# The skip term of an S4D convolution: VectorE adds for groups of chunks in place of TensorE products for each chunk

## The chip, the cores and the metric

The kernel runs on one core of a Trainium2 chip. A core has a matrix engine (TensorE, in the profile PE, its weight loads PEld), VectorE (DVE), ScalarE (ACT), GpSimd (POOL), and a queue engine that issues most transfers (SyncE, SP). Every engine works through its own list of instructions in order; an instruction that needs something of another engine or of a transfer waits on a semaphore, and all that stands behind it on its engine waits too. The metric is the device time of one execution in microseconds, as the median of several runs; a profiled execution gives the trace.

## The reference

A block of a conditioned sequence model: sequence length 2048, width D = 640, 128 complex states per channel, feed-forward width 1728, batch 1, all float32. Cut to what matters:

```python
def ssm(u, log_A_real, A_imag, C_real, C_imag, log_dt, D_skip):   # u: [1, L, D]
    dt = exp(log_dt)
    A = -exp(log_A_real) + 1j * A_imag                            # [D, N]
    C = (C_real + 1j * C_imag) * dt[:, None]
    K = 2 * einsum("dn,dnl->dl", C, exp((A * dt[:, None])[:, :, None] * arange(L))).real
    y = irfft(rfft(u_t, 2 * L) * rfft(K, 2 * L))[..., :L]         # causal convolution
    return y_t + u * D_skip

sa, ca, ga, sb, cb, gb = split(silu(c) @ w_mod, 6)
h = layernorm(x) * (1 + ca) + sa
x = x + ga * ssm(h, ...)
h = layernorm(x) * (1 + cb) + sb
x = x + gb * ((silu(h @ w1) * (h @ w3)) @ w2)
```

The skip term `u * D_skip` is the same as adding `D_skip` to the convolution kernel K at time 0, channel by channel. That is how the kernel does it, before and after the change: it adds `D_skip` to one element of each channel's generated kernel.

## The kernel before

The 640 channels are five blocks of 128 (b = 0 to 4), and a block is eight chunks of 16 channels (c = 0 to 7). For each chunk the convolution kernel K is generated on the chip:

- GpSimd adds up phases as integers (`ph`, task `g{b}.{c}.ph`) and multiplies magnitudes (`yy`, `xx`, tasks `z0` to `z2`).
- ScalarE takes sines and cosines (`tr`, tasks `s0` to `s4`), VectorE multiplies them in (`yy`, `xx`, tasks `m0` to `m4`).
- TensorE sums over the states into PSUM (`kps`, 128 x 256, task `p`, the function `product` inside `gen_chunk`): 64 small products. Then come four more products, each of a 32 x 32 identity with four columns of the table `dsk`, which add `D_skip` to column 63 of each of the chunk's four 64-column groups. `kps` has one buffer.
- ScalarE copies `kps` to the chunk's 256 columns of the block's table `ks` in SBUF (task `r`, function `rows`).

`ks` goes through a two-stage Fourier transform by matmuls. The first stage is eight tasks `k{b}.{i}.m` for a block (in the profile `ps<-wk,ks`, 16 passes each); task i reads the columns of chunk i. Its result is copied to `sp` by VectorE or ScalarE (task `e`). The second stage is `fk`. The normalized input takes a parallel road: `hn`, `hb`, a store to device memory (`hs<-hb`), a load in another layout (`xb<-hs`), the same first stage (`ps<-wk,xb`) and a second one, `fh`. The spectra are multiplied (`hz`, `fp`) and go back by `fz`, `zt` and further transfers (`zd`, `iz`). All this ends near 331 us; the feed-forward part takes the rest, and is bound by TensorE.

`dsk` is a 128 x 160 table, zero but for four partitions, that is filled once near the start by four small loads on SyncE's queue, after the loads of x, of the modulation weights (`sp<-in_w_mod`) and of two constant tables.

What sets the order: each step is a task with an engine and the names of the tasks it needs (`Plan.add`). One long table of numbers, `ORDER`, lists the tasks in the order of issue (an accent picks the second of two engines); `Plan.sequence` checks it against the needs and `InOrder` keeps each engine to it, so that nothing is rearranged later. All instructions that go through `InOrder` show its line, L151. ScalarE also has other work in these lists: squares for the layernorm statistics (`xs<-xs,h_nm`), and for each block five exponentials (`late<-late`) with a table load ahead and another behind.

Of the kernel before, what the change touches and what calls it, by code (L numbers as in the profile page):

```python
# [10 lines left out]
F32 = mybir.dt.float32  # L11
F32R = mybir.dt.float32r
I32 = mybir.dt.int32
AF = mybir.ActivationFunctionType
# [4 lines left out]
P = 128  # L19
# [6 lines left out]
NB = 5  # L26
E4 = P // 4
# [7 lines left out]
1 80 78 81 79 82 83 150' 2 4 19 42 20 41 14 21 15 84 22 43 23 44 16 85 151 24 17 25 26 45 46 18 28 59 47 30 27 29 48 96 33 36 49  # L35
34 5 111 35 32 61 31 37 40 50 51 38 39 3 152' 153 156 6 7 8 52 53 62 60 157 154 10 91 158 155 159 167 168 89 86 120 93 87 95 107
54 121 13 310 105 109 98 169 171 113 172 173 110 106 90 174 55 102 100 88 56 114 176 118 177 183 179 66 170 117 178 184 185 57 104
58 64 187 188 108 175 99 189 180 181 67 186 192 194 9 115 193 103 190 160 92 199 200 201 101 97 203 11 195 68 202 161 182 204 191
215 122 123 208 65 63 209 196 197 69 205 206 210 116 94 207 211 219 112 138 124 127 198 162 212 71 213 128 134 400' 119 163 125
# [3 lines left out]
267 338 334 259 339 315 265 266 405 260 268 77 335' 409 72 147 148 149 0 550 340 272 273 269 274 270 271 261 275 322 330 279 276  # L43
555 283 280 281 288 341' 551' 262 282 284 285 323 286 331 290 552 289 553 318 277 326 556 319 287 291 327' 417 421 418 422 278 320
321 423 292 557 426 545 316 293 137 410 75 74 546 424 419 558 420 427 317' 428 547 548 328 413' 414 324 429 425 294 329 430 433
437 325 346 342 344 554 559 436 434 442 435 431 347 438 444 343 345' 443 348 350 365 352 439 549 440 441 432 445 449 450 451 452
# [12 lines left out]
730 752 753 608 399 630 826 744 745 618 757 756 827 754 631 755 619 641 759 750 763 764 758 620' 760 766 765 767 768 746 769 770  # L59
# [2088 lines left out]
```

## Time and profile before

| | before |
|---|---|
| median of 3 runs | 940.48 us (939.96 to 941.41) |
| the profiled execution's own time | 940.2 us |
| its span | 938.4 us |
| mean granted TensorE clock | 0.983 |
| instructions | 21120 |
| TensorE busy | 856.7 us (91%) |
| VectorE busy | 693.8 us (74%) |
| ScalarE busy | 539.7 us (58%) |
| GpSimd busy | 342.3 us (36%) |
| share of the chain that ended last: TensorE, VectorE, transfers, ScalarE, GpSimd | 70%, 12%, 6%, 5%, 3% |

The shares are means over the whole span, and the two parts of the program are unlike: up to about 331 us all engines are busy with the convolution, after about 375 us TensorE alone is. So the tables by stretch, and the chain of waits piece by piece, say more than the busy shares. In a row of the timeline stand the start and the length of an instruction or a run of like ones (us), engine, line, operation, output and inputs, and in brackets how long the engine stood before it and what released it. A row of the chain has start, length, engine or transfer, output.

### The profile page before, as it was taken

The page shows a single profiled execution, that of the slowest core. Times are in us where ns is not written, and L with a number is a line of the kernel's source. Part 1 is how long each engine was busy: PE and PEld are TensorE (multiplying, and loading weights), DVE is VectorE, ACT ScalarE, POOL GpSimd, SP SyncE. Part 2 cuts the span into 40 slices and gives each one's busy share as a digit, 9 for nine tenths or more (in the row PEclk, how much of TensorE's full clock was granted, in tenths as well). Part 3 has the DMA queues.
Part 4 walks back from the last instruction along what each step waited for, and adds up shares of the span by engine and source line. Part 5 has one row for each costly group of instructions (what it writes and reads, how often), then busy time and mean ns, then how long its engine had stood idle before and what let it go on. Part 6 is the DMA issues. An engine that isn't in the chain of part 4 may idle for free.

```text
span 938.4 us, 21120 instructions
## 1 busy us (share of the span) xinstructions
PE 856.7 (91%) x8309; PEld 679.0 (72%) x8309; DVE 693.8 (74%) x1310; ACT 539.7 (58%) x1032; POOL 342.3 (36%) x370
## 2 busy tenths in 40 slices
PE   1167999999999986999999999999999999999997
PEld 1035857878888873787777778878788888888776
DVE  7998999999989977897677676668656464646523
ACT  6789999989787741754344454446444444444311
POOL 0899989998998500002121121000121212120000
PEclk9987999999999998999999999999999999999999
DMA  9976563525143598655354322275532323230274
GB/s 206 267 236 166 160 156 108 135 81 128 48 110 88 137 242 210 167 183 168 110 157 126 116 82 70 85 229 190 148 106 74 95 75 94 73 96 29 90 244 144
DMA packets 110124, 127.40 MB, mean 136 GB/s; under 512 B 10697, under 2 KB 89801, under 8 KB 108745
## 3 DMA queue, kind: packets, MB, share of 16 engines
q1 hardware_dynamic: 108552, 124.88, 46.5%
q8 instruction: 65, 1.06, 0.5%
q10 hardware_dynamic: 1472, 1.18, 0.5%
q14 instruction: 35, 0.28, 0.1%
HBM read 95.89 MB, written 30.15 MB: 134 GB/s over the span
## 4 chain that ended last, share of the span: by engine, by line
PE 70%; DVE 12%; DMA 6%; ACT 5%; POOL 3%; issue 2%; SPq 1%; ACTq 0%; DVEq 0%; POOLq 0%
PE c L151 19%; PE acc L151 17%; PE X L151 12%; PE ps L151 5%; PE fz L151 4%; PE kps L151 3%; PE fk L151 3%; PE fh L151 3%; PE gu L151 2%; DMA zd<-zt 1%; DVE xb L151 1%; PE iy L151 1%; DVE yy L151 1%; DVE xx L151 1%; DMA sp<-zd 1%
## 5 line engine op out<-in xcount | busy, mean ns | idle before, releaser
L151 PE MATMUL acc<-w,ah 128*128 128x512 f32 x448 | 137.0, 391 | 0.8 <-DMA w<-w2d 0.8
L151 ACT ACTIVATE tr<-ph 128x512 f32<-128x512 int32 (+1 forms) x160 | 93.7, 599 | 6.9 <-DVE yy L151 3.6
L151 PEld LDWEIGHTS acc<-w,ah 128*128 128x128 f32 x448 | 83.4, 188 | 18.1 <-ACT ah L596 1.2
L597 DVE TENSOR_TENSOR wl<-s,wh 128x256 fp32r<-128x256 f32 x92 | 39.0, 424 | 65.3 <-ACT wh L596 65.0
L151 PE MATMUL acc<-w,al 128*128 128x512 f32 x208 | 81.3, 391 | 2.0 <-DVE al L597 2.0
L773 POOL TENSOR_TENSOR s<-wr 128x256 f32<-128x256 f32 x22 | 16.5, 748 | 179.2 <-DVE wl L597 111.2
L596 ACT ACTIVATE wh<-s 128x256 fp32r<-128x256 f32 x92 | 37.8, 410 | 75.9 <-PE X L151 56.8
L151 POOL TENSOR_TENSOR ph<-p,p 128x1024 int32<-128x1024 int32 x40 | 78.7, 1968 | 4.7 <-ACT tr L151 4.1
L596 ACT ACTIVATE wh<-wr 128x256 fp32r<-128x256 f32 x92 | 38.3, 418 | 52.2 <-PE X L151 40.1
L774 POOL TENSOR_TENSOR s<-s,wr 128x256 f32<-128x256 f32 x22 | 17.0, 772 | 131.1 <-issue 131.0
L834 ACT ACTIVATE t<-g 128x512 f32<-128x512 f32 x44 | 27.8, 632 | 55.1 <-DVE g L798 55.0
L151 DVE TENSOR_TENSOR yy<-yy,tr 128x512 f32<-128x512 f32 (+1 forms) x60 | 56.6, 945 | 2.8 <-ACT tr L151 1.8
L803 DVE SCALAR_TENSOR_TENSOR g<-t,g 128x512 f32<-128x512 f32 x48 | 33.7, 702 | 31.3 <-ACT t L834 29.4
L151 DVE TENSOR_TENSOR xx<-tr,xx 128x512 f32<-128x512 f32 x80 | 54.2, 681 | 2.3 <-ACT tr L151 1.8
L151 PE MATMUL fz<-fp,wz 64*128 64x512 f32 x224 | 54.1, 608 | 0.4 <-DVE fp L151 0.4
L151 PE MATMUL kps<-yy,xx 128*32 128x64 f32 x1920 | 37.3, 229 | 17.3 <-DVE xx L151 14.2
L151 PEld LDWEIGHTS kps<-yy,xx 128*32 128x32 f32 x1920 | 32.3, 113 | 27.1 <-issue 10.3
L597 DVE TENSOR_TENSOR wl<-wr,wh 128x256 fp32r<-128x256 f32 x92 | 40.5, 441 | 14.4 <-ACT wh L596 14.3
L151 PE MATMUL ps<-wk,xb 128*64 128x128 f32 x640 | 47.5, 294 | 2.9 <-DVE hb L151 0.9
L151 PEld LDWEIGHTS ps<-wk,xb 128*64 128x64 f32 x640 | 43.3, 220 | 5.3 <-issue 1.4
L151 PEld LDWEIGHTS acc<-w,al 128*128 128x128 f32 x208 | 39.0, 188 | 11.1 <-DVE al L597 2.9
L775 POOL TENSOR_TENSOR s<-wr 128x256 f32<-128x256 f32 x22 | 16.9, 769 | 79.8 <-DVE wl L151 48.4
(464 smaller groups left out, 2473.8 us busy)
## 6 DMA issues: line engine op xcount, KB each, us to landing
w<-w2d SPq DMA_DIRECT2D x42, 640.0 KB, 3.9
wr<-in_w SPq DMA_DIRECT2D x50, 320.0 KB, 3.6
zd<-zt SPq DMA_DIRECT2D x40, 256.0 KB, 3.3
w2d<-w SPq DMA_DIRECT2D x14, 640.0 KB, 3.4
xs<-in_x SPq DMA_DIRECT2D x16, 320.0 KB, 11.8
hs<-hb SPq DMA_DIRECT2D x20, 256.0 KB, 3.4
xb<-hs SPq DMA_DIRECT2D x20, 256.0 KB, 4.7
iz<-zd SPq DMA_DIRECT2D x32, 160.0 KB, 4.1
```

The source lines that it names most:

```text
L151: self.prev = self.k.order(f(*a, **kw), self.prev)
L596: self.nc.scalar.activation(H, v, AF.Copy)
L597: eng.tensor_tensor(Lo, v, H.bitcast(F32), op=ALU.subtract)
L773: eng.tensor_tensor(s[0], u[:, 0:2], u[:, 2:4], op=ALU.add)
L774: eng.tensor_tensor(s[1], s[0], g[:, 0:2], op=ALU.subtract)
L775: eng.tensor_tensor(s[2], g[:, 0:2], u[:, 0:2], op=ALU.subtract)
L803: V.scalar_tensor_tensor(g, th, 1.0, g, op0=ALU.add, op1=ALU.mult)
L834: tanh = lambda o, i: A.activation(o, i, AF.Tanh, scale=0.5)
```

## The change

- The four identity products of each chunk go, and the dependence of the chunk's `p` on the `dsk` loads with them.
- `kps` and a new row of 160 columns share one PSUM buffer, `small` (128 x 512): columns 256 to 511 are `kps`, columns 0 to 159 the row.
- A new ScalarE task `dskp` copies the whole table `dsk` to that row, once, after its four loads.
- New VectorE tasks `d{b}.{c}` add the row's columns to column 63 of the 64-column groups of `ks`, for several chunks at once; c is the last chunk of the group. The table `SKIPS` gives the groups: chunks 0 to 3, 4, 5 to 7 in block 0; 0 to 3, 4 to 6, 7 in blocks 1 and 2; 0 to 3, 4 and 5, 6, 7 in blocks 3 and 4. That makes 17 additions of 128 x 16, 12, 8 or 4 elements. Each needs the copies `r` of all chunks of its group, and `dskp`.
- The first-stage transform of a chunk needs its group's addition, where it needed the chunk's own copy.
- `ORDER` is written anew, because the new tasks shift the numbers. Decoded to names, all old tasks stand in their old order on every engine.

```diff
+SKIPS = (((0, 3), (4, 4), (5, 7)), ((0, 3), (4, 6), (7, 7)), ((0, 3), (4, 6), (7, 7)), ((0, 3), (4, 5), (6, 6), (7, 7)), ((0, 3), (4, 5), (6, 6), (7, 7)))
...
-            for q in range(4):
-                g = slice(32 * q, 32 * q + 32)
-                nc.tensor.matmul(kps.rearrange("p (e b) -> p e b", b=64)[g, :, 63], self.ident[g, g], self.dsk[g, d0 // P, d0 % P // 4:d0 % P // 4 + 4],
-                                 start=False, stop=True, skip_group_check=True, tile_position=(32 * q, 32 * q))
...
+        self.small = psg.tile([P, 512], F32, name="small", tag="kg", bufs=1)
...
-                kps[c] = self.psg.tile([P, 256], F32, name=f"kps{b}{c}", tag="kg", bufs=1)
+                kps[c] = self.small[:, 256:]
...
-            add(n + "p", "PE", 1.3, lambda c=c: ch[c][4](), [n + f"m{i}" for i in range(5)] + (["dsk"] if b == 0 else []), t + 3,
+            add(n + "p", "PE", 1.3, lambda c=c: ch[c][4](), [n + f"m{i}" for i in range(5)], t + 3,
...
+        def skip(c0, c1):
+            o, d = slice(4 * c0, 4 * c1 + 4), self.small[:, :NB * E4].rearrange("p (b e) -> p b e", b=NB)
+            V.tensor_add(self.ks[b][:, o, 63], self.ks[b][:, o, 63], d[:, b, o])
+        for c0, c1 in SKIPS[b]:
+            add(f"d{b}.{c1}", "DVE", .2, lambda c0=c0, c1=c1: skip(c0, c1), [f"{g}.{c}.r" for c in range(c0, c1 + 1)] + ["dskp"], base(c1) + 4)
...
-            after = [f"g{b}.{i}.r"] if m else [f"h{b}.f"]
+            after = [f"d{b}.{c1}" for c0, c1 in SKIPS[b] if c0 <= i <= c1] if m else [f"h{b}.f"]
...
+        add("dskp", "ACT", .3, lambda: A.activation(self.small[:, :NB * E4], flat(self.dsk), AF.Copy), ["dsk"], 20)
```

Where the new instructions stand (the operation, output and inputs with the tile's running number, and the shape; the helper's line is one further down after the change). On ScalarE, near the start, among sines (`tr`, `ph`) and the squares for the layernorm statistics, before:

```order
L151 ACTIVATE ph_293<-ph_293 128x1024
L151 ACTIVATE xs_243,h_ss<-xs_243,h_nm 128x640 x2
L151 ACTIVATE xs_260,h_ss<-xs_260,h_nm 128x640
L151 ACTIVATE tr_0_336<-ph_293 128x512
L151 ACTIVATE xs_176,h_nm<-xs_176 128x640 x2
```

and now:

```order
L152 ACTIVATE ph_294<-ph_294 128x1024
L152 ACTIVATE small<-dsk 128x160
L152 ACTIVATE xs_244,h_ss<-xs_244,h_nm 128x640 x2
L152 ACTIVATE xs_261,h_ss<-xs_261,h_nm 128x640
L152 ACTIVATE tr_0_338<-ph_294 128x512
L152 ACTIVATE xs_177,h_nm<-xs_177 128x640 x2
```

The copy of the row (`dskp`) stands ahead of the squares. On VectorE, in the first block, where chunk 4's last products (`tr_64` with `yy` and `xx`) and the normalized input (`hn`, `hb`) alternate, before:

```order
L151 TENSOR_TENSOR xx_641<-tr_64_677,xx_641 128x512
L151 TENSOR_TENSOR yy_642<-yy_642,tr_64_680 128x1024
L151 TENSOR_TENSOR hb_763<-hn,rw 128x512
L151 TENSOR_TENSOR xx_641<-tr_64_682,xx_641 128x512
L151 TENSOR_SCALAR hn<-sp,rs_y_h,rs_n_h 128x128 x4
L151 TENSOR_SCALAR p_118<-pB 128x128
L151 TENSOR_TENSOR hn<-hn,rw 128x512
L151 TENSOR_TENSOR hb_830<-hn,rw 128x512
```

and now:

```order
L152 TENSOR_TENSOR xx_628<-tr_64_664,xx_628 128x512
L152 TENSOR_TENSOR yy_629<-yy_629,tr_64_667 128x1024
L152 TENSOR_TENSOR ks_132<-ks_132,small 128x16
L152 TENSOR_TENSOR hb_746<-hn,rw 128x512
L152 TENSOR_TENSOR xx_628<-tr_64_669,xx_628 128x512
L152 TENSOR_SCALAR hn<-sp,rs_y_h,rs_n_h 128x128 x4
L152 TENSOR_TENSOR ks_132<-ks_132,small 128x4
L152 TENSOR_SCALAR p_119<-pB 128x128
L152 TENSOR_TENSOR hn<-hn,rw 128x512
L152 TENSOR_TENSOR hb_809<-hn,rw 128x512
```

The additions for chunks 0 to 3 and for chunk 4 stand ahead of `hb` and of `p`. On VectorE, in the second block, between the products of chunk 7 (`tr_240`) and copies of first-stage results (`sp<-ps`), before:

```order
L151 TENSOR_TENSOR hb_2067<-hn,rw 128x512
L151 COPY sp_917<-ps_2069 128x64x8
L151 TENSOR_TENSOR yy_1880<-yy_1880,tr_240_2055 128x1024
L151 COPY sp<-ps_2164 128x64x8
L151 TENSOR_TENSOR xx_1879<-tr_240_2057,xx_1879 128x512
```

and now:

```order
L152 TENSOR_TENSOR hb_2003<-hn,rw 128x512
L152 COPY sp_896<-ps_2005 128x64x8
L152 TENSOR_TENSOR yy_1821<-yy_1821,tr_240_1991 128x1024
L152 TENSOR_TENSOR ks_1305<-ks_1305,small 128x12
L152 COPY sp<-ps_2096 128x64x8
L152 TENSOR_TENSOR xx_1820<-tr_240_1993,xx_1820 128x512
```

The addition for chunks 4 to 6 stands ahead of the copy of `ps_2096`, which is the first-stage transform of chunk 5.

More of the change, by code (lines that the diff above doesn't have):

```diff
@@ L34 @@
 ORDER = """
[L35 to L38, printed above, removed]
@@ new lines @@
+289 345' 558' 263 283 285 286 327 287 335 291 559 290 560 322 278 330 563 323 288 292 331' 421 425 422 426 279 324 325 427 293 564
+430 552 320 294 138 414 76 75 553 428 423 565 424 431 321' 432 554 555 332 417' 418 328 433 429 295 333 434 298 437 441 329 350 346
+348 561 566 440 438 446 439 435 351 442 448 347 349' 447 352 354 369 356 443 556 444 445 436 449 453 454 455 456 457 458 450 462 469
[3 rows of a table added]
+817 818 549 387 506 391 393 395 507 392 498 1067 814 375 508 518 389 396 511 512 510 499 394 397 589 513 509 500 521 1068 398 590'
@@ new lines @@
+514 577 522 519 661 659 533 520 534 535 581 820 377 819 1069 578 537 515 591 528 527 1070 526 579 582 523 821' 822 823 1072 1071 388
[7 rows of a table added]
+752 625 802 764 763 837 761 638 762 626 648 766 757 770 771 765 627' 767 773 772 774 775 753 776 777 926 644 645 649 629 781 780 768
+646 628 617 650 779 782 778 647 783 786 790 769 791 787 923 789 927 792 1339 639 630 651 795 1340 784 793 642 788 1180 640 797 1341
+796 846 1342 798 847' 840 844 841' 794 785 845' 803 1345' 935 939 936 928 652 944 938 951 937 799 1346 655' 1347 1181 940 643 800
@@ new lines @@
+1367' 1384 1383 1473 1477 1385 1386 1387 1389 1388 1397 1398 1402 1390 1391 1399 1481 1403 1455 1448 1458 1457 1450 1460 1451 1462
+1459 1464 1461 1392 1400 1401 1393 1395 1466 1463 1447 1468 1465 1396 1467 1394 1404 1417 1418 1405 1406 1480 1412 1414 1413 1407
+1475 1408 1415 1409 1469 1470 1416 1482 1419 1427 1429 1420 1421 1428 1483 1410 1432 1433 1434 1430 1431 1422 1443 1489 1435 1436
+1490 1491 1478 1492 1472 1471 1411 1423 1425 1437 1440 1438' 1424 1426 1441 1439 1493 1485 1505 1506 1513 1514 1516 1507 1494 1496
[9 rows of a table added]
```

28 lines of the change are left out of this document (10 added, 18 removed), and 72 rows, old and new, of the table ORDER.

## The prediction

> **What bounds the kernel now.** I read the busy table first, then the windows (engine columns are busy us, the column PEclk the granted clock), then the chain of waits.
>
> ```profile
> PE 856.7 (91%) x8309; PEld 679.0 (72%) x8309; DVE 693.8 (74%) x1310; ACT 539.7 (58%) x1032; POOL 342.3 (36%) x370
> ```
> ```profile
> 47.00:92.00 45.00, 32.15 (x596) 20.19 (x596) 39.89 (x79) 40.57 (x78) 42.93 (x42) 0.82 0.72 203
> ...
> 105.00:127.00 22.00, 20.33 (x442) 16.85 (x444) 20.97 (x27) 19.88 (x38) 18.10 (x16) 1.00 0.41 118
> ...
> 147.00:170.00 23.00, 20.83 (x429) 17.08 (x419) 21.79 (x40) 21.56 (x37) 21.72 (x23) 1.00 0.58 143
> ...
> 375.00:938.00 563.00, 551.88 (x2459) 443.12 (x2457) 356.81 (x713) 251.14 (x503) 66.69 (x88) 1.00 0.40 123
> ```
>
> The 91% for PE is a mean over two different kernels. From 375 us on PE works 551.88 of 563 us and this change touches nothing there: that part moves as a block. All forty chunks lie before 331 us, and there VectorE, ScalarE and GpSimd are as full as PE: 39.89, 40.57 and 42.93 of 45 us against PE's 32.15 in the stretch 47 to 92. So the first third is a chain that changes hands:
>
> ```profile
> 52.03 0.69 DVE x L151
> ...
> 81.22 3.64 DMA hs<-hb
> ...
> 105.05 2.84 PE ps L151 x48
> 107.89 1.27 PE kps L151 x68
> ...
> 325.39 1.29 PE kps L151 x69
> ```
>
> A reader should see two things. PE's `kps` steps, the ones that lose work, lie on the chain only from 107.89 on (that row and the one at 325.39 are the first and last of 24). Before that the chain runs over VectorE, ScalarE and transfers, and those get the new work and the new waits. Since every engine runs its list in order, what counts is less the price of an add than whether its operands are there when its place in the list comes.
>
> **What is removed.** One chunk's four skip products (eight passes) take the step from their start to the next matmul:
>
> ```profile
> 306.56 0.24 PE L151 MATMUL kps<-dsk,ident 32*32 32x4 f32 x8
> 306.73 1.99 PE L151 MATMUL fz<-fp,wz 64*128 64x512 f32 x8
> ```
>
> 306.73 - 306.56 = 0.17 us, so 40 x 0.17 = 6.8 us of PE time, but 24 x 0.17 = 4.1 us on the chain. Four of the 24 lie ahead of the wait at 162 us below, where PE ends up waiting for other engines whatever it did before; I count 20 x 0.17 = 3.4 us, with 0 and 4.1 as ends.
>
> **Term A: ScalarE waits for the skip row to land.** The copy of the row into PSUM (task `dskp`) stands in ScalarE's list after the 34.54 step and ahead of the squares at 37.82, and needs the four `dsk` transfers.
>
> ```profile
> 22.63 3.29 SPq L151 DMA_DIRECT2D sp<-in_w_mod  x3
> 27.07 6.06 SPq L151 DMA_DIRECT2D dsk<-in_d_skip  x4
> ```
> ```profile
> 36.27 1.93 PE L151 MATMUL pm<-sp,sc 128*32 128x512 f32 x8 [12.30 <-DMA sp<-in_w_mod]
> 38.52 1.61 PE L151 MATMUL pm<-sp,sc 128*32 128x512 f32 x8 [0.32 <-DMA sp<-in_w_mod]
> ```
> ```profile
> 40.00:41.00 1.00, 0.77 (x7) 0.42 (x4) 1.00 (x3) 1.00 (x4) 1.00 (x2) 1.00 0.02 8
> ```
> ```profile
> 34.54 1.06 ACT L151 ACTIVATE ph<-ph 128x1024 f32<-128x1024 int32 x1
> 37.82 0.83 ACT L151 ACTIVATE xs<-xs,h_nm 128x640 f32<-128x640 f32 x1 [2.22 <-DVE h_nm L151]
> ...
> 45.81 0.83 ACT L151 ACTIVATE xs<-xs,h_nm 128x640 f32<-128x640 f32 x1 [0.34 <-DVE h_nm L151]
> ```
>
> The `dsk` issues end at 33.13 (27.07 + 6.06), behind three large loads of modulation weights on the same queue. PE's waits date the first two of these: 36.27 and 38.52, so 2.25 us apart; the third comes at about 40.8 and the row behind it. The transfers' share falls to 0.02 in 40 to 41, so little is left by then. Estimate of the landing: 41.2, between 40.3 and 42. The copy takes at most the 0.37 us of a 128x256 one (the 79.55 row below), so the squares begin near 41.5 instead of 37.82: 3.7 us, less the 0.34 us that ScalarE waits at 45.81. VectorE takes it over where it waits for ScalarE, the 52.03 step of the chain. **A = +3.4 us**, 2.5 to 4.2.
>
> [...]
>
> **Term B: the first add waits for chunk 3 of block 0.** The add for chunks 0 to 3 stands between `yy` (74.93) and `hb` (76.05, right behind it), that for chunk 4 ahead of `p` (78.91).
>
> ```profile
> 74.93 1.21 DVE L151 TENSOR_TENSOR yy<-yy,tr 128x1024 f32<-128x1024 f32 x1
> ...
> 76.66 0.68 DVE L151 TENSOR_TENSOR xx<-tr,xx 128x512 f32<-128x512 f32 x1
> ...
> 78.91 0.97 DVE L151 TENSOR_SCALAR p<-pB 128x128 int32<-128x128 int32 x1
> ...
> 81.94 0.69 DVE L151 TENSOR_TENSOR x<-x,tr 128x512 f32<-128x512 f32 x1 [0.74 <-ACT tr L151]
> ...
> 89.23 0.30 DVE L151 TENSOR_SCALAR cols<-pv 128x5 f32<-128x5 f32 x3 [1.73 <-PE pv L151]
> ```
> ```profile
> 75.94 3.71 ACT L151 ACTIVATE late<-late 128x1024 f32<-128x1024 f32 x5
> 79.55 0.37 ACT L151 ACTIVATE ks<-kps 128x256 f32<-128x256 f32 x1
> ```
>
> Chunk 3's copy runs behind five exponentials and ends at 79.92. VectorE reaches the add at 76.05 and stands 3.87 us, plus the add's 0.2: 4.1. Queued behind it are `xx` (chunk 4's last product, now ending near 81.4 instead of 77.3), and `hb`, whose store is the chain's 81.22 step. Chunk 4's `kps` follows `xx`, takes 1.5 us (the 80.02 row below) and its copy 0.37, so it ends near 83.4; the next add's place comes at 78.91 + 4.1 = 83.0: another 0.4, and 0.2 for the add. VectorE is 4.7 us late at `p`. It has 0.74 + 1.73 = 2.5 us of waits before 92, which take some of it if their releasers don't move as well, though the `hb` store precedes them on the chain. Between 2.2 and 4.7 I take the middle: **B = +3.4 us**.
>
> **Terms C, D, E: transforms that wait for an add.** The first-stage kernel transforms (`ps<-wk,ks`) now need the group's add.
>
> ```profile
> 107.20 0.68 DVE L151 SCALAR_TENSOR_TENSOR yy<-yy,tr 128x512 f32<-128x512 f32 x1
> ```
> ```profile
> 162.73 1.05 PE L151 MATMUL ps<-wk,ks 128*64 128x128 f32 x16
> 165.34 1.09 PE L151 MATMUL ps<-wk,ks 128*64 128x128 f32 x16 [1.57 <-ACT ks L151]
> ```
> ```profile
> 163.82 0.69 DVE L151 COPY sp<-ps 128x512 f32<-128x512 f32 x1 [0.17 <-PE ps L151]
> ```
> ```profile
> 160.33 3.72 ACT L151 ACTIVATE late<-late 128x1024 f32<-128x1024 f32 x5
> ...
> 164.91 0.39 ACT L151 ACTIVATE ks<-kps 128x256 f32<-128x256 f32 x1
> ```
> ```profile
> 270.80 3.34 PE L151 MATMUL ps<-wk,ks 128*64 128x128 f32 x58
> ```
> ```profile
> 273.67 0.67 DVE L151 SCALAR_TENSOR_TENSOR yy<-yy,tr 128x512 f32<-128x512 f32 x1
> ```
> ```profile
> 318.25 1.09 PE L151 MATMUL ps<-wk,ks 128*64 128x128 f32 x16
> ```
> ```profile
> 318.40 0.38 ACT L151 ACTIVATE ks<-kps 128x256 f32<-128x256 f32 x1
> ```
>
> C: the transforms at 105.05 (chunks 7, 5, 6 of block 0) need an add that stands ahead of the `yy` at 107.20. With its 0.2 us PE starts near 107.4, 2.35 us later, and in order, so the `kps` of the chain waits too. PE has 22 - 20.33 = 1.7 us idle in that stretch: between 0.7 and 2.4; PE goes straight on along the chain, so **C = +2.2 us**.
>
> D: the transform at 162.73 is chunk 5 of block 1, and its add covers chunks 4 to 6. Chunk 6's copy, again behind exponentials, ends at 165.30; with the add 165.5, PE is 2.8 us late there, but had 1.57 us of waiting at 165.34, so 1.2 remains directly. VectorE loses more: its place for that add is before the 163.82 copy, which itself reads the late transform (165.5 + 1.0), so it comes at 166.7, 2.9 us late, with 21.79 of 23 us busy and little to absorb it; chunk 7's add is behind this work and the transform that needs it follows at once. **D = +3.1 us**, 1.2 to 3.3.
>
> E: the last quarter of the 270.80 group, chunk 6 of block 3 at about 273.1, needs an add ahead of 273.67 (273.9 with it): 0.8. The 318.25 transform, chunk 4 of block 4, shares an add with chunk 5, whose copy ends at 318.78; 319.0 with the add: 0.75. **E = +1.6 us**, 0 to 3.2 (twice it, as these groups' later adds also come close behind their copies).
>
> **The adds themselves.** None of this kind is in the trace; the nearest are small VectorE operations of 128x16:
>
> ```profile
> 63.52 0.17 DVE L151 SCALAR_TENSOR_TENSOR rs_y_h<-rsw,rs_w_h 128x16 f32<-128x16 f32 x1
> 63.73 0.17 DVE L151 SCALAR_TENSOR_TENSOR rs_n_h<-h_nm,rs_y_h 128x16 f32<-128x16 f32 x1
> ```
>
> Dependent ones follow each other at 0.21 us; one with nothing to wait for costs perhaps 0.07 (the queue hides the rest). Seven adds are inside B to E. The other ten come after their copies and cost 0.7 to 2.1 us of a VectorE that is nearly full until 331: I take +1.4.
>
> **The sum** is made against the profiled execution's own 940.2 (span 938.4, 1.8 around it); the median of the runs is 940.48, 0.3 more. 3.4 + 3.4 + 2.2 + 3.1 + 1.6 + 1.4 - 3.4 = +11.7, so from the median **952.2 us** (951.9 from the profiled one). All low ends: 2.5 + 2.2 + 0.7 + 1.2 + 0 + 0.7 - 4.1 = +3.2 (943.7). All high ends: 4.2 + 4.7 + 2.4 + 3.3 + 3.2 + 2.1 - 0 = +19.9 (960.4).
>
> **The rivals.**
>
> *The row lands early.* If the 0.6 KB row isn't held up by the loads ahead, the copy fits into the 2.22 us that ScalarE idles before 37.82. 952.2 - 3.4 = **948.8**. For it: the issue ends at 33.13. Against: one queue, and a 12.30 us wait for the first load. Chance 0.10.
>
> *GpSimd is the pace: faster.* In 47 to 92 GpSimd works 42.93 of 45 us, in 147 to 170 21.72 of 23, and the change gives it nothing. If it sets when ScalarE and VectorE go on up to 170, A to D fall into time in which they would wait for it anyway. Left are E, the adds' 0.7 and the whole saving: 1.6 + 0.7 - 4.1 = -1.8, **938.7**. It decides as soon as GpSimd's inputs are late by no more than its own idle time (2.1 us in 47 to 92). Against: A alone is 3.4 us, and the chain at 81 to 108 runs over stores and PE. Chance 0.07, of it 0.02 with no change that can be told.
>
> *The waits are mostly absorbed.* PE has 12.85 us idle in 47 to 92; if the terms go toward their low ends, **943 to 946**. Chance 0.06.
>
> *PE gets cold.* After a 2.45 us wait one `kps` took 1.51 us, where the step at 107.89 takes 1.27 with its skip products and so 1.1 without; the granted clock of that stretch is 0.82:
>
> ```profile
> 80.02 1.51 PE L151 MATMUL kps<-yy,xx 128*32 128x64 f32 x64 [2.45 <-ACT ks L151]
> ```
>
> The new waits at C and D are as long. If each costs 0.4 us and the terms go to their high ends: **over 957.5**. Chance 0.05. [...]
>
> **How the numbers follow.** The forecast's own case, the sum within its bounds, has 0.72. With the early row it fills 946.0 to 957.5: 0.82. Below lie the absorbed waits (0.06) and the GpSimd case (0.07), above the cold PE (0.05). A measurement of this kernel can tell about 0.2% (1.9 us) from no change: faster 0.05, same 0.02, slower 0.72 + 0.10 + 0.06 + 0.05 = 0.93.
>
> **What the profile after would show.** A: ScalarE's `small<-dsk` near 41, the wait before it put down to the `dsk` transfer. B: VectorE's first add idle about 3.9 us, released by ScalarE's `ks`. C and D: idle of 2 us or more on PE before transforms that read `ks`, released by VectorE's `ks`, where ScalarE's was the releaser before; PE's busy time lower by about 6 us. From the last fh on, every step later by about the same 11 to 12 us. I am wrong if the adds don't wait (then it is faster), or if the lateness at 110 us is gone by 170 us.

## The result, and the profile after

| | before | after |
|---|---|---|
| median | 940.94 us (939.96 to 942.42, 6 runs) | 952.39 us (950.68 to 955.20, 6 runs) |
| ratio | 1 | 1.0117, 95% interval 1.0100 to 1.0133 |
| span of the profiled execution | 938.4 us | 950.9 us |
| mean granted TensorE clock | 0.983 | 0.973 |

The change makes the kernel 1.17% slower, 11.0 us (9.4 to 12.5). The forecast was 952.2 us.

The page's busy table of the changed kernel, and its windows (the same stretches as before):

```profile
PE 855.5 (90%) x7989; PEld 678.0 (71%) x7989; DVE 694.1 (73%) x1327; ACT 540.5 (57%) x1033; POOL 342.3 (36%) x370
```
```profile
47.00:92.00 45.00, 26.42 (x442) 16.43 (x444) 36.65 (x77) 39.58 (x77) 35.96 (x34) 0.72 0.59 178
92.00:105.00 13.00, 8.61 (x145) 7.21 (x143) 9.33 (x19) 8.09 (x14) 12.54 (x16) 0.80 0.63 124
...
147.00:170.00 23.00, 21.72 (x336) 15.72 (x336) 21.72 (x36) 22.64 (x42) 21.77 (x24) 1.00 0.62 165
...
375.00:938.00 563.00, 549.03 (x2461) 441.26 (x2460) 360.65 (x742) 251.48 (x504) 67.52 (x89) 0.99 0.42 127
```

No engine has noticeably more to do: VectorE's busy time is 694.1 us against 693.8, ScalarE's 540.5 against 539.7. In 47 to 92 all of them do less than before, PE 26.42 us in place of 32.15. So the loss is waiting. Its places, first ScalarE, then VectorE, then ScalarE again:

```profile
41.78 0.31 ACT L152 ACTIVATE small<-dsk 128x160 f32<-128x160 f32 x1 [5.94 <-DMA dsk<-in_d_skip]
42.02 0.81 ACT L152 ACTIVATE xs<-xs,h_nm 128x640 f32<-128x640 f32 x1
```
```profile
78.72 1.21 DVE L152 TENSOR_TENSOR yy<-yy,tr 128x1024 f32<-128x1024 f32 x1
84.15 0.18 DVE L152 TENSOR_TENSOR ks<-ks,small 128x16 f32<-128x16 f32 x1 [4.22 <-ACT ks L152]
84.25 0.68 DVE L152 TENSOR_TENSOR hb<-hn,rw 128x512 f32<-128x512 f32 x1
...
88.12 0.16 DVE L152 TENSOR_TENSOR ks<-ks,small 128x4 f32<-128x4 f32 x1 [0.92 <-ACT ks L152]
...
89.10 0.69 DVE L152 TENSOR_TENSOR hb<-hn,rw 128x512 f32<-128x512 f32 x1
...
103.18 1.77 DVE L152 TENSOR_SCALAR hn<-xq,rs_y_h,rs_n_h 128x128 f32<-128x128 f32 x4 [2.47 <-DMA xq<-in_x]
```
```profile
83.75 0.37 ACT L152 ACTIVATE ks<-small 128x256 f32<-128x256 f32 x1
```

The row lands at 41.78, the squares begin 4.20 us later than before (42.02 against 37.82). VectorE reaches its first addition at 79.93 and stands 4.22 us until chunk 3's copy (83.75, behind the exponentials) is done; the second `hb`, at 80.50 before, comes at 89.10. That lateness reaches VectorE a second time: SyncE issues the loads of `xq` behind the stores of `hb` and the loads of `xb`, from 95.85 us on in place of 86.72, and VectorE waits 2.47 us for them (103.18), a wait that the kernel before does not have. And TensorE, which now waits for additions:

```profile
101.30 5.41 PE L152 MATMUL ps<-wk,xb 128*64 128x128 f32 x48 [3.52 <-DMA xb<-hs]
...
117.15 4.37 PE L152 MATMUL ps<-wk,ks 128*64 128x128 f32 x48 [2.60 <-DVE ks L152]
```
```profile
178.74 3.43 PE L152 MATMUL ps<-wk,ks 128*64 128x128 f32 x32 [2.86 <-DVE ks L152]
...
185.63 1.97 PE L152 MATMUL ps<-wk,ks 128*64 128x128 f32 x32 [1.25 <-DVE ks L152]
...
289.20 1.09 PE L152 MATMUL ps<-wk,ks 128*64 128x128 f32 x16 [1.24 <-DVE ks L152]
...
333.43 1.09 PE L152 MATMUL ps<-wk,ks 128*64 128x128 f32 x16 [1.04 <-DVE ks L152]
```

These are the terms C (2.60), D (2.86 and 1.25) and E (1.24 and 1.04) of the prediction, at the transforms it named. The passes behind the long waits are slow as well: 48 take 4.37 us at C, where the kernel before takes 2.84 (its row at 105.05), and 32 take 3.43 us at D, where it takes 1.05 and 1.09 (its rows at 162.73 and 165.34). The section on the cold clock comes back to this.

How the lateness builds up is seen best on one engine. The table follows VectorE's own old instructions, which stand in the same order in every kernel: how much later than in the profile before (us) the same instruction starts, by the timelines. The columns behind the first are experiments of the next section; each column is one execution.

| VectorE's instruction, at (before) | after | best | only_row | only_first_add | early_pair | only_three_chunks | only_block1 | no_skip |
|---|---|---|---|---|---|---|---|---|
| `x`, 52.03 | 3.77 | 0.71 | 3.44 | 0.99 | 3.00 | 0.52 | 0.69 | 0.09 |
| `hb`, 80.50 | 8.59 | 0.54 | 3.26 | 5.21 | 8.10 | 0.35 | 0.52 | 0.43 |
| `xx`, 92.38 | 6.46 | 2.06 | 5.41 | 3.36 | 5.96 | 2.70 | 2.10 | 1.00 |
| `yy`, 107.20 | 9.82 | 2.31 | 5.65 | 5.42 | 8.43 | 2.78 | 2.35 | 1.00 |
| `fp`, 112.18 | 13.19 | 2.31 | 5.65 | 5.42 | 8.43 | 4.70 | 2.35 | 1.00 |
| `hn`, 165.02 | 16.95 | 4.11 | 5.96 | 5.69 | 10.24 | 5.11 | 7.45 | 2.04 |
| `yy`, 305.03 | 14.52 | 1.74 | 3.20 | 4.04 | 7.69 | 3.78 | 5.09 | -0.27 |
| `late`, 362.26 | 13.82 | 0.26 | 1.89 | 2.81 | 6.23 | 2.38 | 4.44 | -1.32 |
| `mv`, 370.02 | 11.30 | -2.52 | -0.89 | 0.02 | 3.44 | -0.41 | 1.65 | -4.10 |

In the column after, 3.8 us come at the row and 4.8 more at the first additions. VectorE's own waits take 2.1 us back by 92 us (8.59 to 6.46), and 3.4 return by 107 us, most of them in the wait for `xq`. Then 3.4 more come at the three chunks (9.82 to 13.19) and 3.7 more in block 1 (162 us, 13.20, to 16.95). How far one execution can be trusted: best and only_blocks34 are the same program up to block 3, yet at 165.02 the one stands at 4.11 and the other at 2.90, so a difference of 1.2 us between two columns can come without any edit. From 305 us to the last row every column falls by 3 to 4.5 us, that without the skip term too (-0.27 to -4.10), so this part says more of the one execution profiled before than of the change; why, stays open.

### The profile page after: what moved, and what is told of

The parts are those of the page before. It is cut to its first block, busy times and chain, and to the rows that moved or that the text cites. A ratio compares the mean times of both kernels' runs of the same rounds, so it can differ in the third digit from the quotient of the medians.

```text
span 950.9 us, 20498 instructions
## 1 busy us (share of the span) xinstructions
PE 855.5 (90%) x7989; PEld 678.0 (71%) x7989; DVE 694.1 (73%) x1327; ACT 540.5 (57%) x1033; POOL 342.3 (36%) x370
## 4 chain that ended last, share of the span: by engine, by line
PE 55%; DVE 3%; DMA 1%; ACT 1%; SPq 0%; issue 0%; ACTq 0%; DVEq 0%
PE c L152 19%; PE acc L152 17%; PE X L152 12%; PE gu L152 3%; PE iy L152 1%; PE tp L152 1%; DMA w<-w2d 1%; DVE oc L994 1%; PE gh L152 0%; DMA izb<-zd 0%; SPq L1013 0%; PE fz L152 0%; DVE x L1005 0%; DMA zd<-zt 0%; DVE oc L1487 0%
## 5 line engine op out<-in xcount | busy, mean ns | idle before, releaser
L770 POOL TENSOR_TENSOR s<-wr 128x256 f32<-128x256 f32 x22 | 16.6, 754 | 181.9 <-DVE wl L594 76.7
L152 PE MATMUL small<-yy,xx 128*32 128x64 f32 x1920 | 38.1, 233 | 23.5 <-DVE xx L152 23.4
L152 PEld LDWEIGHTS small<-yy,xx 128*32 128x32 f32 x1920 | 33.1, 115 | 32.5 <-issue 22.4
L152 PE MATMUL ps<-wk,ks 128*64 128x128 f32 x640 | 44.2, 293 | 9.4 <-DVE ks L152 9.0
L594 DVE TENSOR_TENSOR wl<-wr,wh 128x256 fp32r<-128x256 f32 x92 | 40.5, 441 | 14.5 <-ACT wh L593 14.5
L152 PEld LDWEIGHTS ps<-wk,ks 128*64 128x64 f32 x640 | 38.7, 148 | 14.4 <-DVE ks L152 10.0
```

The costliest lines, as they stand in the source:

```text
L152: self.prev = self.k.order(f(*a, **kw), self.prev)
L594: eng.tensor_tensor(Lo, v, H.bitcast(F32), op=ALU.subtract)
L770: eng.tensor_tensor(s[0], u[:, 0:2], u[:, 2:4], op=ALU.add)
```

## The experiments

The theory: the time is lost where an in-order engine reaches a new instruction before its operands. The first rival, load: VectorE is nearly full, and each addition costs some 0.7 us by itself. The second, the cold clock: the new gaps slow TensorE down. All ratios are to the kernel before, measured beside it. Its median was 940.45 us in some of these measurements and 941.82 or 942.29 in others, so rows are compared by their ratios and not by their medians.

| run | what it is | median, us | ratio (95%) |
|---|---|---|---|
| after | the change | 952.39 | 1.0117 (1.0100 to 1.0133) |
| no_skip | before, without the skip products (the skip term is left out) | 938.57 | 0.9963 (0.9945 to 0.9980) |
| best | change, additions well placed | 940.48 | 0.9982 (0.9966 to 0.9998) |
| row_late | change, A undone | 947.86 | 1.0062 (1.0039 to 1.0085) |
| no_first_wait | change, B undone | 948.75 | 1.0065 (1.0044 to 1.0086) |
| only_row | best, A put back | 942.68 | 1.0004 (0.9991 to 1.0017) |
| only_first_add | best, B put back | 940.73 | 1.0000 (0.9986 to 1.0014) |
| early_pair | best, A and B put back | 945.99 | 1.0039 (1.0021 to 1.0058) |
| only_three_chunks | best, C put back | 941.83 | 1.0019 (1.0005 to 1.0032) |
| only_block1 | best, D put back | 942.99 | 1.0021 (1.0004 to 1.0038) |
| only_blocks34 | best, E put back | 939.40 | 0.9990 (0.9979 to 1.0001) |
| adds_four_times | best, each addition four times (the skip term counts four times) | 948.39 | 1.0066 (1.0045 to 1.0088) |
| warm | change, TensorE busy in one gap | 953.83 | 1.0111 (1.0081 to 1.0140) |

A difference of two ratios is turned into microseconds by 941 us; it is uncertain by 2 to 3 us (both half intervals, added as squares).

### The floor: no skip term

```diff
-            for q in range(4):
-                g = slice(32 * q, 32 * q + 32)
-                nc.tensor.matmul(kps.rearrange("p (e b) -> p e b", b=64)[g, :, 63], self.ident[g, g], ...)
```

> The kernel before without the four skip products of each chunk and with nothing in their place: it leaves out the skip term. It measures the saving alone. The theory of waits (the time of the change is lost where an engine reaches a new instruction before its operands) has the saving at 20 to 24 steps of 0.17 us on the chain: 2 to 4 us off 940.9, so 937 to 939. The theory of load (VectorE is nearly full before 331 us, so each of the 17 additions costs some 0.7 us, through its own time and through a PSUM bank that it shares with TensorE's products) says the same of this run; it is needed as the floor for the other three.

Measured: 0.9963, 3.5 us less (1.9 to 5.2). The saving is real and of the size taken, 3.4. The table's last column shows where it comes in this execution: from 2.04 us late at 165 to 0.27 early at 305, that is 2.3 us over the stretch where TensorE's `kps` steps are on the chain. The 2 us lost ahead of it come in two places: 1.0 by 92 us, where ScalarE is late (it begins chunk 3's five exponentials at 77.41 against 75.94), and 1.0 more between 125 and 131 us. What delays them in this execution stays open.

### Well-placed additions

The row's copy and all additions that waited, in lists by task names (an `m` task is a product, `n`, `x`, `a` make `hn` and `hb`, `e` is a copy of a transform):

```diff
-SKIPS = (((0, 3), (4, 4), (5, 7)), ((0, 3), (4, 6), (7, 7)), ..., ((0, 3), (4, 5), (6, 6), (7, 7)))
+SKIPS = (((0, 3), (4, 4), (5, 7)), ((0, 3), (4, 5), (6, 6), (7, 7)), ..., ((0, 3), (4, 4), (5, 5), (6, 6), (7, 7)))
 ScalarE
-g0.0.s2  dskp  sq22 ... g0.0.s4  sq11
+g0.0.s2  sq22 ... g0.0.s4  dskp  sq11
 VectorE, block 0
-g0.4.m3  d0.3  h0.1.a  g0.4.m4  h0.2.n  d0.4  t1.0.3  h0.2.x  h0.2.a  g0.5.m1  g0.5.m2
+g0.4.m3  h0.1.a  g0.4.m4  h0.2.n  t1.0.3  h0.2.x  h0.2.a  d0.3  g0.5.m1  g0.5.m2  d0.4
-h1.0.x  h1.0.a  g1.0.m3  g1.0.m4  d0.7
+h1.0.x  d0.7  h1.0.a  g1.0.m3  g1.0.m4
 VectorE, block 1
-k1.3.e ... g1.7.m3  d1.6  k1.5.e  g1.7.m4  h3.3.n  g2.0.m0  h3.3.x  g2.0.m2  d1.7
+d1.5  k1.3.e ... g1.7.m3  k1.5.e  g1.7.m4  d1.6  h3.3.n  g2.0.m0  h3.3.x  d1.7  g2.0.m2
 VectorE, blocks 3 and 4
-g3.7.m4  k3.5.e  d3.6  g4.0.m0  k3.6.e  d3.7  g4.0.m1  g4.0.m2  g4.0.m3
+d3.6  g3.7.m4  k3.5.e  g4.0.m0  k3.6.e  g4.0.m1  g4.0.m2  d3.7  g4.0.m3
-z3.3.v1  d4.5  g4.6.m0  g4.6.m2  g4.6.m3  k4.4.e ... k4.3.e  d4.6  g4.7.m3
+z3.3.v1  d4.4  g4.6.m0  g4.6.m2  g4.6.m3  d4.5  k4.4.e ... k4.3.e  g4.7.m3  d4.6
```

> The changed kernel with its new instructions placed where their operands are there: the copy of the row as in the run before; the additions for chunks 0 to 3 and 4 of block 0 behind the second hb and the product that follow them; that for chunks 5 to 7 one hb earlier; block 1 in groups 0 to 3, 4 and 5, 6, 7 and block 4 in groups 0 to 3, 4, 5, 6, 7, each behind its copy; blocks 3 and 4 likewise. That makes 19 additions in place of 17, and the same work. By the theory of waits all of A to E goes but for some 0.5 us, and what is left is the saving of 2 to 4 us less 1 to 2 us for additions: 938 to 940.5, at or below the kernel before. By the theory of load it stays well above: 19 x 0.7 us less the saving, 948 to 952.

Measured: 0.9982 (0.9966 to 0.9998). This decides between the two: two more additions than the change has, and 12.7 us less time. Load is out as the cause. What is left of the waits in its trace (ScalarE's copy, two of VectorE's additions, the same transforms on TensorE):

```profile
46.12 0.29 ACT L152 ACTIVATE small<-dsk 128x160 f32<-128x160 f32 x1
```
```profile
83.00 0.19 DVE L152 TENSOR_TENSOR ks<-ks,small 128x16 f32<-128x16 f32 x1 [1.27 <-ACT ks L152]
...
221.13 0.17 DVE L152 TENSOR_TENSOR ks<-ks,small 128x12 f32<-128x12 f32 x1
221.21 1.75 DVE L152 TENSOR_SCALAR hn<-xq,rs_y_h,rs_n_h 128x128 f32<-128x128 f32 x4
```
```profile
107.33 2.84 PE L152 MATMUL ps<-wk,ks 128*64 128x128 f32 x48 [0.47 <-DVE ks L152]
...
169.26 1.09 PE L152 MATMUL ps<-wk,ks 128*64 128x128 f32 x16 [2.01 <-DVE ks L152]
```

The copy of the row has no wait ahead of it, the three chunks' transforms wait 0.47 us in place of 2.60; the 2.01 us at 169.26 stand where 1.57 us of waiting for chunk 6's copy stood before. An addition that waits for nothing holds VectorE 0.08 us (221.13 to 221.21); its row is 0.17 us long, so the next instruction begins before it ends. Of the versions that compute everything this has the lowest ratio, 0.18% below the kernel before, with an interval that just leaves out 1; the gain is small.

### Term A, undone and alone

```diff
 row_late (in the change)
-g0.0.s2  dskp  sq22 ... g0.0.s4  sq11
+g0.0.s2  sq22 ... g0.0.s4  dskp  sq11
 only_row (in best)
-g0.0.s2  sq22 ... g0.0.s4  dskp  sq11
+g0.0.s2  dskp  sq22 ... g0.0.s4  sq11
```

> The changed kernel with one instruction moved: ScalarE copies the skip row seven entries of its list later, ahead of the square that waited for VectorE at 45.81 us in the kernel before. The transfers have landed by then. By the theory of waits, term A goes: the 5.94 us wait of ScalarE before the copy shrinks to its old 2.22 us wait, VectorE's first addition comes 3.4 to 3.8 us earlier, and the time falls from 952.4 to 948.5 to 949.5. If early lateness of ScalarE is made up later on (VectorE still has 2.5 us of waits before 92 us), or by the theory of load, it stays at 951 to 952.5.

> The kernel of the run before with one thing put back: the row's copy at the place that the change gave it, so ScalarE waits for the transfers at about 36 to 41.8 us. Term A alone. By the theory of waits 3.4 us above that run (2.5 to 4.2), and no wait of VectorE for the additions. If ScalarE's early lateness is made up before 331 us: less than 1 us above it.

Undone, A gives back 0.0055, 5.2 us; alone it costs 0.0022, 2.1 us. The wait itself is what was predicted:

```profile
41.44 0.31 ACT L152 ACTIVATE small<-dsk 128x160 f32<-128x160 f32 x1 [5.44 <-DMA dsk<-in_d_skip]
```

Each figure is uncertain by 2 to 3 us; the first is above what was expected (2.9 to 3.9), the second below it (3.4). The wait is 5.44 us here, and VectorE is 2.7 us later than in best at `x` (3.44 against 0.71), 3.3 at 92 to 107, and 1.5 to 1.6 from 305 us on. The rival of an early row is out: the row lands at 41.4 to 41.8 us, 8.5 us after its last issue.

A part of the 5.2 us is not A's own. Behind the wait at C, 2.62 us long in row_late, the 48 passes take 2.84 us there and not the 4.37 of the change, and VectorE's step between 107.20 and 112.18 is 1.9 us (6.41 to 8.33) in place of 3.4: in that profile the clock did not fall at C (1.00 in 105 to 127 us, 0.88 in the change). That is 1.5 us of the difference between the two executions.

### Term B, alone, undone, and with A

```diff
 only_first_add (in best); early_pair has this and dskp ahead of sq22
-g0.4.m3  h0.1.a  g0.4.m4  h0.2.n  t1.0.3  h0.2.x  h0.2.a  d0.3  g0.5.m1  g0.5.m2  d0.4
+g0.4.m3  d0.3  h0.1.a  g0.4.m4  h0.2.n  d0.4  t1.0.3  h0.2.x  h0.2.a  g0.5.m1  g0.5.m2
 no_first_wait (in the change): the reverse
```

> The kernel with well-placed additions (the run best, 940.5), with one thing put back: the additions for chunks 0 to 3 and 4 of block 0 stand ahead of hb and p as in the change. Term B alone. The prediction took 3.4 us between 2.2 and 4.7, by the middle. The trace of the changed kernel has VectorE 4.8 us later at the second hb than at the yy ahead of the first addition, and the store that follows, the loads and TensorE's first transforms of xb just as late; so if the chain of stores carries all of it: 4.2 to 5 us above best, 944.7 to 945.5. If VectorE's waits absorb their part: 2.2 to 3.4 us, 942.7 to 943.9. By the theory of load nothing changes: 940.5.

> The run best with two things put back together: the row's copy early on ScalarE (term A) and the additions for chunks 0 to 3 and 4 ahead of hb and p (term B). Alone they cost 2.1 and 1.7 us. If the terms add, 3.8 us above best: 944.3. If each alone hides in the same slack of VectorE before 92 us and the two together exceed it, or if the longer gap lets TensorE's clock drop at the first transforms of xb (5.41 us for 48 passes in the changed kernel, 3.53 before), 5.5 to 7 us above: 946 to 947.5.

> The changed kernel with term B alone undone: the additions for chunks 0 to 3 and 4 behind the second hb and the product after it. If the terms add, 1.7 us under the changed kernel: 950.7. If B costs more in the company of A, as above: 3.4 to 5 us under it, 947.4 to 949, and the first transforms of xb take 3.5 us again.

Alone 0.0018, 1.7 us, which its uncertainty of 2 us does not distinguish from nothing and which is less than the theory of waits expected; taken out of the change, 0.0052, 4.9 us; with A, 0.0057, 5.4 us, where the two alone make 3.8. The addition waits as in the change, and VectorE waits for `xq`:

```profile
80.77 0.18 DVE L152 TENSOR_TENSOR ks<-ks,small 128x16 f32<-128x16 f32 x1 [3.61 <-ACT ks L152]
...
98.80 1.77 DVE L152 TENSOR_SCALAR hn<-xq,rs_y_h,rs_n_h 128x128 f32<-128x128 f32 x4 [1.19 <-DMA xq<-in_x]
```

By the table VectorE is 4.7 us later than best at the second `hb` (5.21 against 0.54), yet 1.3 at 92.38, where A alone is 3.3 later and the pair 3.9. So on VectorE itself most of B's lateness is taken in by waits that it has between 81 and 92 us anyway, among them the 0.74 and 1.73 us that the prediction had counted.

But the stores and loads keep it: SyncE issues the loads of `xq` from 92.13 us on, 86.72 before, VectorE waits 1.19 us for them, and at 107.20 the three stand 3.3, 3.1 and 6.1 above best. There the two add. In the last row they stand 1.6, 2.5 and 6.0 above best. That the pair keeps its lateness and each alone loses a part can't be put down to the edits: in 127 to 147 us the granted clock is 0.91 in best and in early_pair, and 1.00 in the two others, so best, from which all three are counted, lost time there that A alone and B alone did not. The medians leave 1.6 us of interplay, with an uncertainty of about 3 us: that B costs more in company isn't shown.

### Terms C, D and E alone

```diff
 only_three_chunks (in best)
-h1.0.x  d0.7  h1.0.a  g1.0.m3  g1.0.m4
+h1.0.x  h1.0.a  g1.0.m3  g1.0.m4  d0.7
 only_block1, only_blocks34 (in best): block 1, or blocks 3 and 4, in the groups and at the places of the change
```

> The run best with one thing put back: the addition for chunks 5 to 7 of block 0 stands ahead of the yy product as in the change, some 2.2 us later than in best. Term C alone. By the theory of waits TensorE stands 2.0 to 2.4 us ahead of the three transforms and the time is 1.9 to 2.4 us above best: 942.4 to 942.9. If the 1.7 us that TensorE has idle in the 22 us behind it take it in: 0.7 us above, 941.2.

> The run best with one thing put back: block 1 in the groups 0 to 3, 4 to 6, 7 at the places of the change. Term D alone. By the theory of waits chunk 5's transform waits for chunk 6's copy behind the exponentials, VectorE's next copy waits for that transform, and chunk 7's addition comes late too: 3.1 us above best, 943.6 (2.5 to 3.3). If TensorE's own lateness counts alone (2.8 us less the 1.57 us that it waited before): 1.2 us above, 941.7.

> The run best with one thing put back: the additions of blocks 3 and 4 in the groups and places of the change. Term E alone: 1.6 us above best by the prediction, 942.1 (0 to 3.2). If the wait for the last transfers before 375 us gives it back, as the trace of the changed kernel shows for the sum (15.7 us late at the first fh after 326 us, 12.5 us at the end): under 0.5 us above best.

C costs 0.0037, 3.5 us; D 0.0039, 3.7 us; E 0.0008, 0.8 us. The rows of TensorE, a fence for each of the three runs; the second has a row of VectorE behind it:

```profile
110.12 2.84 PE L152 MATMUL ps<-wk,ks 128*64 128x128 f32 x48 [2.60 <-DVE ks L152]
```
```profile
169.24 3.34 PE L152 MATMUL ps<-wk,ks 128*64 128x128 f32 x32 [2.81 <-DVE ks L152]
...
176.13 1.97 PE L152 MATMUL ps<-wk,ks 128*64 128x128 f32 x32 [1.25 <-DVE ks L152]
```
```profile
171.26 0.69 DVE L152 COPY sp<-ps 128x512 f32<-128x512 f32 x1 [2.08 <-PE ps L152]
```
```profile
275.77 1.09 PE L152 MATMUL ps<-wk,ks 128*64 128x128 f32 x16 [1.24 <-DVE ks L152]
...
320.01 1.09 PE L152 MATMUL ps<-wk,ks 128*64 128x128 f32 x16 [1.04 <-DVE ks L152]
```

C: the wait is 2.1 us longer than the 0.47 us in best, and nearly all of that passes on; in the table the lateness steps by 1.9 (2.78 to 4.70) at the place where best has no step, and the `yy` of 107.20 is only 0.5 us later than in best. D: the step at 165 is 3.3 us above best (7.45 against 4.11), by the longer way, over VectorE. Of it 0.9 us is slow passes: VectorE's copy of chunk 5's transform comes at 171.26, 2.02 us after the transform begins, where before it came 1.09 us after (162.73 and 163.82). E: two gaps of 1.24 and 1.04 us, of which 0.8 us is left in the time (not distinguished from nothing).

The five put back one at a time make 2.1 + 1.7 + 3.5 + 3.7 + 0.8 = 11.8 us. The change is 0.0135, 12.7 us, above best. So the five waits account for the difference within the uncertainty, which is wide here, about 7 us, because best's own enters with every term. VectorE's table says the same from single executions: in its last row A, B, C and D alone stand 1.6, 2.5, 2.1 and 4.2 us above best, E 0.9, together 11.3, and the change 13.8.

### The price of an addition

```diff
-            V.tensor_add(self.ks[b][:, o, 63], self.ks[b][:, o, 63], d[:, b, o])
+            for _ in range(4):
+                V.tensor_add(self.ks[b][:, o, 63], self.ks[b][:, o, 63], d[:, b, o])
```

> The run best with every addition done four times in a row, so that the skip term is counted four times; 57 more additions at 19 places. It prices an addition by itself. The prediction had 0.07 us (hidden issue) to 0.21 us (dependent steps of 128x16 operations), on a VectorE that is busy nine tenths of the time before 331 us: 57 x 0.07 to 0.21 = 4 to 12 us if all of it comes through, and 940.5 + 4 to 8 if VectorE's gaps take a third. By the theory of load (0.7 us for each addition, PSUM bank shared with TensorE) 40 us. That the kernel best is 1.8 us above the kernel without the skip term says 0.1 for each: 6 us, 946.5.

Measured: 0.0084 above best, 7.9 us (5.4 to 10.4), 0.14 us for each of the 57. In the trace four of them in a row hold VectorE 0.80 us, each dependent on the one ahead:

```profile
224.96 0.80 DVE L152 TENSOR_TENSOR ks<-ks,small 128x12 f32<-128x12 f32 x4
225.76 0.41 DVE L152 TENSOR_SCALAR hn<-xq,rs_y_h,rs_n_h 128x128 f32<-128x128 f32 x1
```

Three more are so some 0.63 us, 12 us at 19 places, and two thirds of it show. That puts an addition of the change below 0.2 us, with its PSUM operand and the shared buffer. Nor does the shared buffer hold TensorE up: in the change its products into `small` wait for VectorE's `xx` (23.4 us in all) and ScalarE's copies (1.1 us), and for no addition.

### The cold clock

```diff
+            if b == 0 and m and i == 4:
+                add("warm", "PE", 2.8, lambda: [again(4) for _ in range(3)], [n + "m"], t)
 TensorE, in the change
-k0.4.m  g0.5.p  hh0.3.m
+k0.4.m  g0.5.p  warm  hh0.3.m
```

> The changed kernel with TensorE kept at work in the gap of 3.52 us ahead of the first transforms of xb: the transform of chunk 4 of block 0 is done three times more into the same bank, 48 passes of 58 ns, which only a copy of VectorE waits for, that has slack until the transfer of xq lands. No other instruction moves. If the gap lets the clock drop (the cold rival of the prediction): the 48 passes fall from 5.41 us to near 3.5, and the time by 1 to 2 us, to 950.5 to 951.4. If the clock has another reason, or the lateness passes to other engines anyway: 5.4 us again or no change in time, 952.4.

The clock comes back, the time doesn't follow. TensorE in this run, and its window (0.80 in the change):

```profile
98.89 2.84 PE L152 MATMUL ps<-wk,ks 128*64 128x128 f32 x48
102.16 3.31 PE L152 MATMUL ps<-wk,xb 128*64 128x128 f32 x48 [0.44 <-DMA xb<-hs]
```
```profile
92.00:105.00 13.00, 10.99 (x207) 9.31 (x206) 9.50 (x18) 9.11 (x16) 12.70 (x14) 1.00 0.62 143
```

The 48 passes take 3.31 us in place of 5.41. The ratio, 1.0111 (1.0081 to 1.0140), isn't distinguished from the change's. Between 92.38 and 112.18 VectorE falls 6.7 us further behind in the change (6.46 to 13.19) and 5.8 here (7.63 to 13.46), so by these two executions about 1 us was to be had at this place; VectorE also waits for `xq` there, 2.47 and 1.88 us. That the clock fell because of the gap is shown by one execution of each; a part of this gap in the 11 us isn't, and is under some 4 us by the two intervals.

The run fills one gap only. The clock falls behind the waits at C and D too: in the change it is 0.50 in 116.92 to 120.33 us and in 178.36 to 181.77, in this run 0.92 over 105 to 127 us, the stretch with C. In the profile of the change the stretches at 0.50 between 70 and 125 us are 6.8, 6.8, 6.8 and 3.4 us long (72.55 to 79.37, 82.79 to 89.60, 99.86 to 106.68, 116.92 to 120.33). Around the wait at C, which is 2.60 us long in both, two stretches of 3.4 us of the change and two of only_three_chunks:

```profile
113.50:116.92 3.42, 1.05 (x18) 0.86 (x14) 3.39 (x5) 2.81 (x6) 3.42 (x3) 1.00 0.76 230
116.92:120.33 3.41, 3.18 (x30) 3.18 (x32) 0.80 (x4) 1.09 (x2) 2.40 (x3) 0.50 0.63 159
```
```profile
105.54:108.95 3.41, 1.98 (x32) 1.79 (x28) 3.38 (x6) 3.38 (x8) 3.41 (x4) 1.00 0.95 312
108.95:112.36 3.41, 2.24 (x41) 2.24 (x43) 1.71 (x4) 1.34 (x4) 3.41 (x3) 1.00 0.78 219
```

In the change most of the wait lies in one stretch, in which TensorE is busy for 1.05 us, and the next stretch has half the clock; in only_three_chunks the wait is divided between two, with 1.98 and 2.24 us of work, and the clock stays. The 48 passes take 4.37 us in the one and 2.84 in the other, and VectorE's step between 107.20 and 112.18 is 3.4 us against 1.9. (It is 3.5 in no_first_wait and 3.2 here, both with a clock of 0.92 over 105 to 127 us, and 1.9 in row_late, with 1.00.) With the 0.9 us at D this makes some 2.4 us of lateness by slow passes at C and D in the profiled execution of the change. How many of its other executions have it, and so how much of the 11 us it is, stays open.

## Why the prediction was right

| step of the prediction | taken | range | alone | taken out of the change |
|---|---|---|---|---|
| A, the row's landing | +3.4 | 2.5 to 4.2 | 2.1 | 5.2 |
| B, first additions | +3.4 | 2.2 to 4.7 | 1.7 | 4.9 |
| C, three chunks | +2.2 | 0.7 to 2.4 | 3.5 | not run |
| D, block 1 | +3.1 | 1.2 to 3.3 | 3.7 | not run |
| E, blocks 3 and 4 | +1.6 | 0 to 3.2 | 0.8 | not run |
| the other additions | +1.4 | 0.7 to 2.1 | 1.8 for all 19 and what is left of their waits (best against no_skip) | |
| the saving | -3.4 | -4.1 to 0 | -3.5 | |
| sum | +11.7 | 3.2 to 19.9 | 11.8 + 1.8 - 3.5 = 10.1 | 11.0 measured |

The mechanism of the waits is the one predicted, at all five places: each wait is in the trace with the releaser named. The wait of ScalarE (41.78 against the estimate of 41.2), that of VectorE (4.22 against 3.87, since ScalarE was late already), those of TensorE at C and D (2.60 and 2.86 against 2.35 and 2.8) came out within 0.6 us.

That the sum came within 0.2 us of the median is in part luck. Measured alone, A, B and E are 1.3, 1.7 and 0.8 us less than taken, C and D 1.3 and 0.6 us more, each uncertain by 2 us; and slow passes at C and D, which the sum put at nothing, make some 2.4 us in the profiled execution.

What was off, step by step:

- **A and B were priced as if each passed on its middle.** Alone they pass on less (2.1 and 1.7), taken out of the change more (5.2 and 4.9). That VectorE's 2.5 us of waits before 92 us "take some of it" was right for VectorE itself, but the stores and loads carried B's lateness past them, to the wait for `xq`. Of what A costs more in the change, 1.5 us is the slow clock at C by the profiles; the rest, and whether the two share the same waits, isn't shown.
- **C was taken at 2.2 with 1.7 us of idle time on TensorE as a way out.** It measured 3.5 with some 2 us of uncertainty. In the profile the wait grows by 2.1 us and VectorE's lateness by 1.9: idle time behind the gap took little of it in, since what follows is itself on the chain.
- **The second addition** waited 0.92 us, not 0.4: chunk 4's products took 1.96 us at a clock of 0.50 (82.79 to 89.60 us) where 1.5 was taken.
- **"From the last fh on, every step later by the same 11 to 12 us"** was wrong. VectorE is 14.5 us late at 305 us and 11.3 at 370. The kernel without the skip term shows the same fall, so it is no give-back of this change's lateness, but the statement failed as it stood.
- **"PE's busy time lower by about 6 us"** came out as 1.2 (856.7 to 855.5). Without the skip products and without the new waits it is 7.0 lower (849.7 in no_skip); in the change slow passes bring much of that back: 1.9 us at the first `xb`, 1.5 at C and 1.3 at D.
- **The cold clock** had a chance of 0.05 as the way to more than 957.5, with 0.4 us for each of the waits at C and D. It happened there, with 1.5 and 0.9 us of VectorE's lateness in the profiled execution, and at the first `xb` besides (a granted clock of 0.80 in 92 to 105, 5.41 us for 48 passes, about 1 us). The total stayed below 957.5 because the other terms did not go to their high ends. That the gaps at C and D add nothing by the clock, as the sum has it, was the author's estimate, and the runs are divided: behind 2.60 us at C 48 passes took 2.84 us in only_three_chunks and 4.37 in the change. The row of 80.02, 1.51 us behind a gap of 2.45, pointed to the second: slow passes followed gaps of 3.52 us in the change but also of 2.60 us at C and of 2.71 us with B alone, where the window of 92 to 105 us has a clock of 0.87:

```profile
97.39 4.71 PE L152 MATMUL ps<-wk,xb 128*64 128x128 f32 x48 [2.71 <-DMA xb<-hs]
```

The rivals on the other side fell as predicted: GpSimd as the pace would have hidden A to D, and GpSimd itself had less to do in 47 to 92 (35.96 us against 42.93), because it, too, waits for what ScalarE and VectorE make (5.5 us for `tr` and 3.2 for `p` in that stretch, 0.9 and 0.4 before). The row that lands early is refuted by the 5.94 us wait, released by the `dsk` transfer: by the issues of the changed kernel,

```profile
27.33 5.98 SPq L152 DMA_DIRECT2D dsk<-in_d_skip  x4
```

which end at 33.31, the row came 8.5 us after the last of them. That it lands behind the loads was the author's estimate, from the one queue and the 12.30 us wait; no run moved the loads ahead of it, so what holds it up isn't shown.

## What to carry to other kernels

Where every engine runs a fixed list, the price of moving a small operation to another engine is not its duration but how early its place comes: ask of each new instruction when its last operand is there, and what stands behind it. A group that saves instructions ties its first reader to its last writer; 17 additions of 0.08 to 0.2 us cost 11 us by that, and 19 well-placed ones cost nothing that the saving didn't cover. Four transfers of 0.6 KB, issued behind three loads of 960 KB on the same queue, were here 8.5 us later than their issue (33.31 to 41.78): the first reader of such a transfer belongs far behind it, as in best, where the copy at 46.12 has no wait. And a wait on TensorE cost more than its length in the profiled execution of the change: behind the 2.60 us at C 48 passes took 4.37 us at a clock of 0.50, and 2.84 at 1.00 in only_three_chunks behind a wait as long.

## What the runs showed of the hardware

The granted clock of TensorE varies from one kernel to the next by amounts that move single rows by 0.5 to 2 us. The same 64 products of chunk 4 took 1.51 us before after a wait of 2.45 us, and in the kernel that only leaves work out

```profile
81.49 1.96 PE L151 MATMUL kps<-yy,xx 128*32 128x64 f32 x64 [3.82 <-ACT ks L151]
```

1.96 us after 3.82 us. Before, the clock is 0.99 in 77.20 to 80.62 us and 0.51 in 80.62 to 84.03, and the products begin at 80.02, so a part of them has the full clock. Here it is 0.88 over 78 to 92 us, as before, and ScalarE's copy comes 1.5 us later (81.02 against 79.55); that the slow stretch lies at the same place, so that all of them fall into it, is the author's estimate from these times.

The first 48 passes of `xb` took 3.53, 3.31 and 3.31 us after waits of 0.56, 0.44 and 1.88 us (before, warm, early_pair), and 4.43, 4.71 and 5.41 us after 2.30, 2.71 and 3.52 us (row_late, only_first_add, the change). The pairs at C show that the length of the wait alone does not decide it. That is why terms of 1 to 2 us are read here from the medians of many runs, and the profiles mainly for what waits for what.
